# Retention attention inside a fused three-stage kernel: decay factors applied to the queries on GpSimd, outputs copied by ScalarE, the state recurrence as one scan, and one sequence of background weight pieces

## The chip, the cores and the metric

The kernel runs on one core of a Trainium2 chip. The metric is device time in microseconds (us) of one execution. TensorE multiplies matrices (PE in the profile, PEld for its weight loads), VectorE (DVE), ScalarE (ACT) and GpSimd (POOL) work elementwise, and SyncE (SP) issues most of the DMAs. Each engine takes its instructions in program order.

## The reference, cut to what matters

Three layers follow each other: attention with a decay, a gated layer (w_in, w_sg, w_out) and a two-matrix layer (w_ch1, w_ch2). B is 4, there are 8 heads, 576 positions, 64 features per head, 512 in all. The lines that the change touches:

```python
scores = scale * np.matmul(q, k.transpose(0, 1, 3, 2))
gamma = 1.0 - 2.0 ** (-5.0 - np.arange(H))
Dmat = np.where(rel >= 0, gamma[:, None, None] ** rel[None, :, :], 0.0)
attn = np.matmul(scores * Dmat, v)
h = gelu(x @ w_in);  u, v = halves of h;  v_n = layernorm(v) * g_ln
x = x + (u * (einsum(w_sg, v_n) + b_sg)) @ w_out
```

The decay is a power of gamma of the distance, so it splits into a factor of the query's position and one of the key's. The weights w_in, w_out and w_ch arrive as 64-bit floats and are turned into 32-bit ones on the chip.

## The kernel before, in words

**Attention.** A unit is one batch entry and one pair of heads: 16 units, `n` from 0 to 15. A unit's queries and keys (transposed), keys and values lie in one tile `ld` of 1120 KB with four buffers. Positions are cut into four chunks of 128 and a rest of 64. `prep_unit` scales the keys by their factors on ScalarE (L212). `scores` multiplies queries and keys on TensorE (L224, L236), and VectorE multiplies the scores by a mask with the keys' factors (L229, L237). `states` forms a key-value product for each chunk (L245) and the running state `y` over chunks: ScalarE copies the first (L251), three VectorE instructions, one behind the other, add the others (L253). `attend` adds both parts of the output on TensorE (L277, L284, L290), and VectorE multiplies it by the queries' factors `grow` on the way from PSUM to `xb` (L295, L300).

**Order.** The loop's iteration `n` issues the load of unit n+3, `prep_unit(n+2)`, `scores(n+1)`, `states(n+1)` and `attend(n)`. Between them stand `background` steps, three in an iteration from n = 2: `f64_pieces` loads 64-bit weights two pieces ahead (L134), converts a piece in four steps on VectorE (L142, L146, L149, L151) with a square on ScalarE (L148), and then splits it into a high and a low part (L310 on ScalarE, L311 on GpSimd) or stores it. w_in, w_sg, w_out and w_ch follow each other; w_out's pieces and w_ch's are two such sequences, and the second issues its first loads when the first has ended. Later the numbers in `PACE` say how many background steps stand behind each tile.

**The gated layer.** For each batch entry `b`, `v_tile` forms the tiles of v and `u_chunk` those of u (L124 to L126), with a gelu on ScalarE (L529) that counts a `tick`; `after(n, fn)` puts work n ticks later. A tile of v is normed (L514, L499, L519 to L523, L526) and split (L554, L555) for `sg_chunk`, which multiplies by w_sg. Where b is even there is a fifth tile, with the rests of two entries: after its norm (L526), two DMAs copy its lower half to `v_rest` (L587), a third overwrites that half (L588), and three ticks later it is split. Before each `u_chunk`, `turn_x` transposes a piece of `xb` on VectorE (L669) and stores it with four DMAs (L676). The tiles of v, the transposed pieces and the rows read back share five buffers `t`, in rotation.

All of these DMAs are issued by SP.

Of the kernel before, what the change touches and what calls it, by code (L numbers as in the profile page):

```python
# [3 lines left out]

# [1 line left out]

# [5 lines left out]
F32 = mybir.dt.float32  # L12
# [3 lines left out]
ALU = mybir.AluOpType  # L16
# [3 lines left out]
B, H, S, D = 4, 8, 576, 64  # L20
E = H * D
NP = H // 2
F1 = 1024
F2 = 2048
C = 128
NC = S // C
# [20 lines left out]
LATE = 6  # L47
# [15 lines left out]
O_GROW = O_MASKR + R  # L63
O_GK = O_GROW + C
O_GC = O_GK + 2
TA = O_GC + 1


O_GLN = 0
# [5 lines left out]
def const_tables():  # L75
    g = np.array(GAMMA, np.float64)
    p = np.arange(128)
    tab = np.zeros((NP, 128, TA), np.float64)
    for hp in range(NP):
        for h in range(2):  # L80
            gh = g[2 * hp + h]
            tab[hp, :, O_MASK + h * C:O_MASK + (h + 1) * C] = (np.arange(C)[None, :] >= p[:, None]) * gh ** -p[:, None]
            tab[hp, :, O_GK + h] = gh ** (C - p)
        gp = g[2 * hp + p // D][:, None]
        tab[hp, :, O_MASKR:O_MASKR + R] = (np.arange(R)[None, :] >= (p % R)[:, None]) * gp ** -(p % R)[:, None]
        tab[hp, :, O_GROW:O_GROW + C] = gp ** np.arange(C)[None, :] / np.sqrt(D)
        tab[hp, :, O_GC] = gp[:, 0] ** C
    return tab.astype(np.float32)


# [1 line left out]
def kernel(  # L92
# [27 lines left out]
    def col(t, o, n=1):  # L120
        return t[:, o:o + n]
# [37 lines left out]
    def bank():  # L159

        return banks.popleft()
# [38 lines left out]
    def prep_unit(n):  # L200
        u = units[n]
        hp = n % NP
        t = u["ld"]
        u["qT"] = t[:, 0:S]
        u["kT"] = t[:, S:2 * S]
        u["k"] = t[:, 2 * S:2 * S + NC * C].rearrange("p (c e) -> p c e", c=NC)
        o = 2 * S + NC * C
        v = t[:, o:]
        u["v"] = v
        for h in range(2):  # L210
            k = u["k"][:, :, h * D:(h + 1) * D]
            act.activation(out=k, in_=k, func=ACTF.Copy, scale=col(tab[hp], O_GK + h))  # L212
# [26 lines left out]
    def states(n):  # L239
        u = units[n]  # L240
        us = bank()
        for c in range(NC):
            for h in range(2):
                r = slice(h * D, (h + 1) * D)
                pe.matmul(  # L245
                    us[r, c * D:(c + 1) * D], u["k"][:, c, r],
                    u["v"][:, c * C + h * D:c * C + (h + 1) * D], start=True, stop=True,
                )

        y = u["y"] = pa.tile([128, NC, D], F32, tag="y", name="y")  # L250
        act.copy(y[:, 0], us[:, 0:D])  # L251
        for c in range(1, NC):
            dve.scalar_tensor_tensor(  # L253
                out=y[:, c], in0=y[:, c - 1], scalar=col(tab[n % NP], O_GC), in1=us[:, c * D:(c + 1) * D],
                op0=ALU.mult, op1=ALU.add,
            )
        free(us)

    def attend_rest(n):
# [8 lines left out]
    def attend(n):  # L268
        u = units.pop(n)
        b, hp = divmod(n, NP)  # L270
        grow = col(tab[hp], O_GROW, C)
        o = bank()
        rest, p, v, qT, y = u["rest"], u["p"], u["v"], u["qT"], u["y"]
        for c in range(NC):
            for h in range(2):
                r = slice(h * D, (h + 1) * D)
                pe.matmul(  # L277
                    o[r, c * C:(c + 1) * C], v[:, c * C + h * D:c * C + (h + 1) * D], p[:, h, c],
                    start=(c == 0), stop=(c == NC - 1), skip_group_check=True,
                )  # L280
        for c in range(1, NC):
            for h in range(2):
                r = slice(h * D, (h + 1) * D)
                pe.matmul(  # L284
                    o[r, c * C:(c + 1) * C], y[r, c - 1], qT[r, c * C:(c + 1) * C], start=False, stop=(c == NC - 1),
                    skip_group_check=True,
                )
        for h in range(2):
            r = slice(h * D, (h + 1) * D)
            pe.matmul(  # L290
                rest[r, 64:64 + R], y[r, NC - 1], qT[r, NC * C:], start=False, stop=True, skip_group_check=True
            )
        if hp == 0:
            xb[b] = xbp.tile([128, KE, S], F32, tag="xb", bufs=4, name="xb")
        dve.tensor_tensor(  # L295
            out=xb[b][:, hp, 0:NC * C].rearrange("p (c i) -> p c i", c=NC),
            in0=o.rearrange("p (c i) -> p c i", c=NC),
            in1=grow.unsqueeze(1).to_broadcast([128, NC, C]), op=ALU.mult,
        )
        dve.tensor_tensor(  # L300
            out=xb[b][:, hp, NC * C:], in0=rest[:, 64:64 + R], in1=grow[:, 0:R], op=ALU.mult
        )
        free(o)
        free(rest)

# [15 lines left out]
    def load_w_out():  # L321
        for k in range(KE):
            if k % 2 == 0:
                s = slot("w_out").rearrange("p (k a n) -> p k a n", k=2, a=2)
            t = s[:, k % 2]
            wo.append(t)
            yield (w_out[k], t[:, 0], t[:, 1])
# [21 lines left out]
    def f64_pieces(pieces, lead=2):  # L349

        pieces = iter(pieces)
        ahead = deque()

        def load():
            todo = next(pieces, None)
            if todo is not None:
                ahead.append((todo, f64_words(todo[0], 512)))

        for _ in range(lead):
            load()  # L360
        yield
        before = None
        while ahead:
            load()
            todo, raw = ahead.popleft()
            steps = f64_to_f32(raw, 512)
            next(steps)
            yield
            if before is not None:
                split(*before)  # L370
                before = None
            c = yield from steps
            if len(todo) == 3:
                before = (todo[1], todo[2], c)
            else:
                nc.sync.dma_start(out=todo[1], in_=c)
            yield
        if before is not None:
            split(*before)
# [37 lines left out]
    def background_steps():  # L417
        yield from f64_pieces(load_w_in(), 1)
        yield from load_w_sg()
        yield from f64_pieces(load_w_out())  # L420
        yield from f64_pieces(islice(w_ch_pieces, 2 * NF - LATE))

    bg = background_steps()

# [114 lines left out]
    def after(n, fn):  # L539
        late.append((step[0] + n, fn))  # L540
# [16 lines left out]
    def v_tile(b, i, ps=None):  # L557

        if ps is None:
            ps = v_products(b, i)  # L560
        if i == 0:
            vn[b] = tuple(big.tile([128, NC + 1, 512], F32R, tag=f"vn{a}", name=f"vn{a}") for a in "hl")
            if b % 2:
                after(1, lambda: iter([split_v(b, NC, v_rest[b])]))
        t = t1.tile([128, 512], F32, tag="t", bufs=NBT, name="t")

        st = numbers(t1)

        def norm_t():
            yield from squares(st, t, vn[b][0][:, i])  # L570

            def numbers_t():
                root(st, st[:, 1:2], 1.0 / 512, 1e-6)
                yield

            after(1, numbers_t)
            after(2, lambda: newton(st))

            def rest():
                normed(t, st)  # L580
                if i < NC:
                    split_v(b, i, t)
                else:

                    r = v_rest[b + 1] = t1.tile([128, 512], F32, tag="rest", bufs=1, name="v_rest")
                    for h in range(2):
                        nc.sync.dma_start(out=r[h * R:(h + 1) * R], in_=t[R:])  # L587
                    nc.sync.dma_start(out=t[R:], in_=t[0:R])  # L588
                    after(3, lambda: iter([split_v(b, i, t)]))
                yield  # L590

            after(3, rest)

        gelu(t, ps, ps, norm_t, st[:, 0:1])
        background(int(PACE[b][0][i]))
# [69 lines left out]
    def turn_x(b, i):  # L665

        n = 128 if i < NC else R
        t = t1.tile([128, 512], F32, tag="t", bufs=NBT, name="x_t")[:, 0:4 * n]
        dve.transpose(  # L669
            out=t.rearrange("p (q k c) -> p k q c", k=KE, c=32),  # L670
            in_=xb[b][:, :, i * 128:i * 128 + n].rearrange("p k (q c) -> p k q c", c=32),
        )
        at = 0 if i < NC else b % 2 * R
        to = x_dram[y_rows.index((b if i < NC else b | 1, i)), at:at + n]
        for q in range(4):
            nc.sync.dma_start(  # L676
                out=to[:, q * 128:(q + 1) * 128].rearrange("(a j) c -> j a c", j=32),
                in_=t[q * 32:(q + 1) * 32].rearrange("j (a c) -> j a c", c=128),
            )

    def load_x(b, i):
        x_rows[b, i] = t1.tile([128, E], F32, tag="t", bufs=NBT, name="x_r")
# [479 lines left out]
```

## Time and profile before

| | |
|---|---|
| time before, median of 3 runs | 700.74 us (699.19 to 702.92) |
| the profiled execution's own time | 702.03 us |
| its span in the profile | 700.2 us |
| TensorE busy | 668.7 us, 96% of the span |
| VectorE, ScalarE, GpSimd busy | 482.9, 303.2, 341.7 us |

Times in the profile count from the span's start; 1.83 us of the execution's own time lie outside the span. A row's "idle before" is time in which the engine had nothing running, with the work that ended most of it. A busy TensorE is not TensorE at its peak, since its matmuls overlap.

### The profile page before, as it was taken

Reading aid. Unit: us, or ns where it says so; the run is one execution under the profiler, and the core shown is the slowest. Engines: PE = TensorE matmul, PEld = TensorE weight load, DVE = VectorE, ACT = ScalarE, POOL = GpSimd, SP = SyncE. Lnnn points to the kernel's source line nnn. Section 1 sums busy time; section 2 is a strip of 40 time slices with the busy share of each in tenths; the row PEclk is TensorE's granted clock in tenths of the full one; section 3 lists DMA queues with packets and bytes.
Section 4 is the critical chain, followed back from the end, with each engine's and each line's share of the span. In section 5 each row is a group of like instructions: output and inputs, shape, how many; then the busy total and the mean of one; then the engine's idle time right before and its main releaser. Section 6 shows DMA issues by size and latency. Waiting matters only on the chain.

```text
span 700.2 us, 11668 instructions
## 1 busy us (share of the span) xinstructions
PE 668.7 (96%) x4294; PEld 594.4 (85%) x4294; DVE 482.9 (69%) x925; ACT 303.2 (43%) x584; POOL 341.7 (49%) x302
## 2 busy tenths in 40 slices
PE   6977997999999899999999999999999999999997
PEld 4866787989889789989888888888988888898985
DVE  2899775987997987686888676677656654433333
ACT  2344475345446436543444544343535433232221
POOL 0222445633622642993555498445448854445411
PEclk8999998999999999999999999999999999999999
DMA  8898635586596749535465523552641153121132
GB/s 323 288 353 301 201 108 161 155 277 198 167 306 206 226 153 259 161 129 208 166 181 169 147 76 106 186 164 93 190 122 61 64 189 124 61 97 69 30 121 90
DMA packets 61960, 116.96 MB, mean 167 GB/s; under 512 B 6480, under 2 KB 25936, under 8 KB 59984
## 3 DMA queue, kind: packets, MB, share of 16 engines
q1 hardware_dynamic: 61904, 116.23, 51.5%
q8 instruction: 33, 0.54, 0.3%
q14 instruction: 23, 0.19, 0.1%
HBM read 88.16 MB, written 27.26 MB: 165 GB/s over the span
## 4 chain that ended last, share of the span: by engine, by line
PE 55%; DVE 22%; DMA 7%; ACT 7%; issue 5%; POOL 3%; SPq 1%; DVEq 0%; ACTq 0%; POOLq 0%
PE b L124 16%; PE b L126 16%; PE b L125 16%; PE b L698 4%; DVE c L151 2%; DVE c L142 2%; DVE c L149 2%; DVE c L146 2%; DVE p L229 2%; DMA w_dram<-c 1%; DMA ld<-in_attn_dram 1%; DVE y L253 1%; DMA rows<-y_dram 1%; DVE xb L295 1%; DVE x_t L669 1%
## 5 line engine op out<-in xcount | busy, mean ns | idle before, releaser
L124 PE MATMUL b<-fe,w 128*128 128x384 f32 x336 | 114.6, 341 | 1.9 <-DVE h L967 1.1
L766 POOL TENSOR_TENSOR w<-raw_w,w 128x512 fp32r<-128x512 f32 x46 | 62.4, 1356 | 107.3 <-ACT w L765 104.3
L126 PE MATMUL b<-w,h 128*128 128x512 f32 x288 | 114.2, 396 | 0.0
L124 PE MATMUL b<-w,h 128*128 128x512 f32 x288 | 113.7, 395 | 0.0
L125 PE MATMUL b<-w,h 128*128 128x512 f32 x288 | 113.5, 394 | 0.0
L125 PE MATMUL b<-fe,w 128*128 128x384 f32 x336 | 113.3, 337 | 0.0
L126 PE MATMUL b<-fe,w 128*128 128x384 f32 x336 | 113.1, 337 | 0.0
L966 ACT ACTIVATE h<-b 128x384 fp32r<-128x384 f32 x72 | 35.3, 490 | 160.4 <-DVE b L994 122.2
L967 DVE SCALAR_TENSOR_TENSOR h<-b,h 128x384 fp32r<-128x384 f32 x72 | 40.0, 556 | 45.6 <-ACT h L966 45.6
L124 PEld LDWEIGHTS b<-fe,w 128*128 128x128 f32 x336 | 63.0, 188 | 9.5 <-DVE t L989 2.7
L752 POOL TENSOR_TENSOR w<-raw_w,w 128x768 fp32r<-128x768 f32 x23 | 45.8, 1993 | 48.3 <-ACT w L751 44.5
L125 PEld LDWEIGHTS b<-fe,w 128*128 128x128 f32 x336 | 63.1, 188 | 3.6
L126 PEld LDWEIGHTS b<-w,h 128*128 128x128 f32 x288 | 54.1, 188 | 13.1
L126 PEld LDWEIGHTS b<-fe,w 128*128 128x128 f32 x336 | 63.1, 188 | 0.0
L125 PEld LDWEIGHTS b<-w,h 128*128 128x128 f32 x288 | 54.1, 188 | 9.4
L124 PEld LDWEIGHTS b<-w,h 128*128 128x128 f32 x288 | 54.0, 188 | 8.7
L148 ACT ACTIVATE raw<-raw 128x512 f32<-128x512 f32 x44 | 29.9, 680 | 64.1 <-DVE c L146 58.9
L994 DVE TENSOR_TENSOR b<-b,u 128x384 f32<-128x384 f32 x48 | 26.9, 561 | 39.7 <-PE b L126 39.6
L751 ACT CAST w<-raw_w 128x1024 fp32r<-128x1024 f32 (+1 forms) x47 | 44.2, 943 | 12.7 <-POOL raw_w L742 8.0
L499 POOL TENSOR_TENSOR st<-st,par 128x1 f32<-128x1 f32 x36 | 23.0, 640 | 52.4 <-DVE st L498 52.1
L389 POOL TENSOR_TENSOR xt_lo<-xb,xt_hi 128x576 fp32r<-128x576 f32 x16 | 25.0, 1575 | 45.6 <-ACT xt_hi L388 41.4
L752 DVE TENSOR_TENSOR w<-raw_w,w 128x1024 fp32r<-128x1024 f32 x24 | 35.4, 1477 | 13.8 <-ACT w L751 13.8
(140 smaller groups left out, 1619.3 us busy)
## 6 DMA issues: line engine op xcount, KB each, us to landing
ld<-in_attn_dram SPq DMA_DIRECT2D x15, 1120.0 KB, 7.1
raw<-in_w_ch_dram SPq DMA_DIRECT2D x32, 512.0 KB, 4.9
raw_w<-w_dram SPq DMA_DIRECT2D x24, 512.0 KB, 3.8
raw_w<-w_dram SPq DMA_DIRECT2D x46, 256.0 KB, 2.6
w_dram<-c SPq DMA_DIRECT2D x32, 256.0 KB, 2.5
row<-y_dram SPq DMA_DIRECT2D x30, 256.0 KB, 4.4
x_r<-x_dram SPq DMA_DIRECT2D x18, 256.0 KB, 4.4
y_dram<-x_r SPq DMA_DIRECT2D x18, 256.0 KB, 3.0
```

Of the source, the lines that this page charges most:

```text
L124: pe.matmul(ps, lh, rh, start=first, stop=False, skip_group_check=True)
L125: pe.matmul(ps, lh, rl, start=False, stop=False, skip_group_check=True)
L126: pe.matmul(ps, ll, rh, start=False, stop=last, skip_group_check=True)
L148: act.activation(out=f(w1), in_=f(w1), func=ACTF.Square)
L389: pool.tensor_tensor(out=lo[:, k, 0:S], in0=xb[b][:, k], in1=f(hi[:, k, 0:S]), op=ALU.subtract)
L698: pe.matmul(ps, g, wo[k][:, w], start=done[0] == 1, stop=done[0] == 3 * KE, skip_group_check=True)
L751: act.copy(hi, r)
L752: (pool if s and part else dve).tensor_tensor(out=lo, in0=r, in1=f(hi), op=ALU.subtract)
L766: pool.tensor_tensor(out=t[:, 1], in0=raw, in1=f(t[:, 0]), op=ALU.subtract)
L966: act.activation(out=t[:, 0], in_=v, func=ACTF.Relu)
L967: dve.scalar_tensor_tensor(out=t[:, 1], in0=v, scalar=0.0, in1=f(t[:, 0]), op0=ALU.max, op1=ALU.subtract)
L994: dve.tensor_tensor(out=v, in0=v, in1=u, op=ALU.add)
```

## The change

- `prep_unit` multiplies the queries by `grow` in place, on GpSimd (on VectorE for unit 0, in two pieces), in one instruction over 512 columns and one over 64. `attend` then only copies its outputs, on ScalarE.
- `states` writes the products with the chunk as the innermost index, so that a feature's four chunks lie side by side in PSUM, and one `tensor_tensor_scan` of 256 elements forms all states. The factor of each step comes from the table, which grows from 451 to 706 columns per partition; `y` is read with a step of four elements by the matmuls of L284 and L290.
- w_out's pieces and w_ch's form one sequence.
- The three DMAs around `v_rest` are issued by ScalarE.
- The stores of `turn_x` are issued two ticks later.

```diff
-TA = O_GC + 1
+TA = O_GC + NC * D
...
-        tab[hp, :, O_GC] = gp[:, 0] ** C
+        tab[hp, :, O_GC:] = gp ** C * (np.arange(NC * D)[None, :] % NC > 0)
...
+        q, grow = u["qT"], col(tab[hp], O_GROW, C)
+        for x, y in ((0, 2), (2, NC)) if n == 0 else ((0, NC),):
+            part = q[:, x * C:y * C].rearrange("p (c i) -> p c i", i=C)
+            (pool if n else dve).tensor_tensor(
+                out=part, in0=part, in1=grow.unsqueeze(1).to_broadcast([128, y - x, C]), op=ALU.mult
+            )
+        (pool if n else dve).tensor_tensor(out=q[:, NC * C:], in0=q[:, NC * C:], in1=grow[:, 0:R], op=ALU.mult)
...
+        us_c = us[:, 0:NC * D].rearrange("p (e c) -> p c e", c=NC)
...
-                    us[r, c * D:(c + 1) * D], u["k"][:, c, r],
+                    us_c[r, c], u["k"][:, c, r],
...
-        y = u["y"] = pa.tile([128, NC, D], F32, tag="y", name="y")
-        act.copy(y[:, 0], us[:, 0:D])
-        for c in range(1, NC):
-            dve.scalar_tensor_tensor(
-                out=y[:, c], in0=y[:, c - 1], scalar=col(tab[n % NP], O_GC), in1=us[:, c * D:(c + 1) * D],
-                op0=ALU.mult, op1=ALU.add,
-            )
+        y = pa.tile([128, D * NC], F32, tag="y", name="y")
+        u["y"] = y.rearrange("p (e c) -> p c e", c=NC)
+        dve.tensor_tensor_scan(
+            out=y, data0=col(tab[n % NP], O_GC, NC * D), data1=us[:, 0:NC * D], initial=0.0, op0=ALU.mult, op1=ALU.add
+        )
...
-        dve.tensor_tensor(
-            out=xb[b][:, hp, 0:NC * C].rearrange("p (c i) -> p c i", c=NC),
-            in0=o.rearrange("p (c i) -> p c i", c=NC),
-            in1=grow.unsqueeze(1).to_broadcast([128, NC, C]), op=ALU.mult,
-        )
-        dve.tensor_tensor(
-            out=xb[b][:, hp, NC * C:], in0=rest[:, 64:64 + R], in1=grow[:, 0:R], op=ALU.mult
-        )
+        act.copy(xb[b][:, hp, 0:NC * C], o)
+        act.copy(xb[b][:, hp, NC * C:], rest[:, 64:64 + R])
...
-        yield from f64_pieces(load_w_out())
-        yield from f64_pieces(islice(w_ch_pieces, 2 * NF - LATE))
+        yield from f64_pieces(chain(load_w_out(), islice(w_ch_pieces, 2 * NF - LATE)))
...
-                        nc.sync.dma_start(out=r[h * R:(h + 1) * R], in_=t[R:])
-                    nc.sync.dma_start(out=t[R:], in_=t[0:R])
+                        act.dma_start(out=r[h * R:(h + 1) * R], in_=t[R:])
+                    act.dma_start(out=t[R:], in_=t[0:R])
...
-        for q in range(4):
-            nc.sync.dma_start(
...
+        def store():
+            for q in range(4):
+                nc.sync.dma_start(
...
+            yield
+
+
+        after(2, store)
```

## Rows read from the trace of the kernel before

**Rows 1.** The page's busy time (share of the span) by engine.

```profile
PE 668.7 (96%) x4294; PEld 594.4 (85%) x4294; DVE 482.9 (69%) x925; ACT 303.2 (43%) x584; POOL 341.7 (49%) x302
```

**Rows 2.** Windows of attention: length, busy time by engine, granted clock, DMA share, GB/s.

```profile
6.50:19.20 12.70, 9.47 (x109) 8.05 (x108) 4.53 (x12) 3.02 (x9) 0.00 (x0) 0.73 0.96 389
23.12:80.89 57.77, 48.82 (x870) 42.59 (x866) 55.84 (x126) 25.12 (x59) 17.50 (x14) 1.00 0.83 303
```

**Rows 3.** Timeline of TensorE: start, length, first matmuls of scores(1), (3), (4), (15).

```profile
12.43 2.08 PE L224 MATMUL b<-ld 64*128 64x128 f32 x16 [1.65 <-DMA ld<-in_attn_dram]
...
23.13 1.16 PE L224 MATMUL b<-ld 64*128 64x128 f32 x16
27.00 1.16 PE L224 MATMUL b<-ld 64*128 64x128 f32 x16
...
80.82 1.16 PE L224 MATMUL b<-ld 64*128 64x128 f32 x16
```

**Rows 4.** Chain of waits in one iteration: start, length of TensorE's pieces.

```profile
20.79 0.62 PE b L245 x16
...
22.28 0.80 PE b L284 x12
```

**Rows 5.** VectorE's groups of instructions from 23.12 to 80.89 us.

```profile
L253 DVE SCALAR_TENSOR_TENSOR y<-y,tab,b 128x64 f32<-128x64 f32 x34 | 9.5, 278 | 1.1
L295 DVE TENSOR_TENSOR xb<-b,tab 128x512 f32<-128x512 f32 x12 | 8.2, 684 | 0.4 <-PE b L284 0.4
L149 DVE SCALAR_TENSOR_TENSOR c<-raw,c 128x512 uint32<-128x512 uint32 x8 | 7.1, 894 | 0.1
...
L300 DVE TENSOR_TENSOR xb<-b,tab 128x64 f32<-128x64 f32 x12 | 2.6, 214 | 0.0
```

**Rows 6.** Groups of instructions: GpSimd over the span, ScalarE up to 110 us.

```profile
L311 POOL TENSOR_TENSOR w_in<-c,w_in 128x512 fp32r<-128x512 f32 x8 | 10.2, 1273 | 33.2 <-ACT w_in L310 33.2
L652 POOL TENSOR_TENSOR grem<-u,grem 128x64 fp32r<-128x64 f32 x16 | 9.0, 567 | 5.0 <-ACT grem L646 5.0
L529 ACT ACTIVATE t<-b 128x512 f32<-128x512 f32 x5 | 3.0, 598 | 2.1 <-PE b L126 2.1
```

**Rows 7.** DMA issues, median us to landing: 24 to 34, then 45 to 56 us.

```profile
ld<-in_attn_dram SPq DMA_DIRECT2D x2, 1120.0 KB, 7.6
...
ld<-in_attn_dram SPq DMA_DIRECT2D x3, 1120.0 KB, 6.1
```

**Rows 8.** Windows around the two later gaps of TensorE.

```profile
114.00:119.00 5.00, 1.16 (x9) 0.93 (x8) 2.76 (x7) 1.77 (x4) 1.49 (x2) 0.89 0.81 295
119.00:124.50 5.50, 5.00 (x20) 4.65 (x21) 5.05 (x8) 2.73 (x7) 1.45 (x2) 0.50 0.53 149
229.50:233.50 4.00, 1.07 (x4) 0.62 (x5) 3.90 (x7) 3.06 (x6) 3.26 (x2) 1.00 0.99 303
```

**Rows 9.** Timeline of SP's queue around the first gap, then at the second.

```profile
107.86 1.46 SPq L587 DMA_DIRECT2D v_rest<-t  x2
111.22 0.46 SPq L588 DMA_DIRECT2D t<-t  x1
...
224.13 1.11 SPq L587 DMA_DIRECT2D v_rest<-t  x2
227.00 0.46 SPq L588 DMA_DIRECT2D t<-t  x1
```

**Rows 10.** Timelines of ScalarE, VectorE and TensorE at the first gap.

```profile
107.43 0.39 ACT L529 ACTIVATE u<-b 128x288 f32<-128x288 f32 x1
...
111.27 0.41 ACT L529 ACTIVATE u<-b 128x288 f32<-128x288 f32 x1
113.42 0.62 ACT L554 CAST vnh<-t 128x512 fp32r<-128x512 f32 x1 [1.75 <-DMA t<-t]
...
115.67 0.43 DVE L142 TENSOR_SCALAR c<-raw 128x512 uint32<-128x512 uint32 x1 [7.49 <-DMA raw<-in_w_ch_dram]
...
118.76 0.61 PE L124 MATMUL b<-w_sg,vnh 128*128 128x288 f32 x1 [3.84 <-ACT vnh L554]
```

More of the change, by code (lines that the diff above doesn't have):

```diff
@@ L2 @@
 from contextlib import ExitStack
-from itertools import islice
+from itertools import chain, islice
 import numpy as np
@@ L270, in attend @@
         b, hp = divmod(n, NP)
-        grow = col(tab[hp], O_GROW, C)
         o = bank()
@@ L674, in turn_x @@
         to = x_dram[y_rows.index((b if i < NC else b | 1, i)), at:at + n]
-        for q in range(4):
-            nc.sync.dma_start(
-                out=to[:, q * 128:(q + 1) * 128].rearrange("(a j) c -> j a c", j=32),
-                in_=t[q * 32:(q + 1) * 32].rearrange("j (a c) -> j a c", c=128),
-            )
+        def store():
+            for q in range(4):
+                nc.sync.dma_start(
+                    out=to[:, q * 128:(q + 1) * 128].rearrange("(a j) c -> j a c", j=32),
+                    in_=t[q * 32:(q + 1) * 32].rearrange("j (a c) -> j a c", c=128),
+                )
+            yield
+        after(2, store)
     def load_x(b, i):
```

## The prediction, made before the change was run

> **What bounds the kernel now.** I read the busy shares first [rows 1]: TensorE is busy for 96% of the span, so the change can gain only where TensorE is idle or at the lower clock, and it can lose wherever it makes TensorE wait. Next I cut attention into stretches [rows 2]. From 23.12 to 80.89 us VectorE is busy for 55.84 of 57.77 us and TensorE for 48.82: here VectorE sets the pace. TensorE's timeline shows what that costs [rows 3]. Between scores(3) and scores(4), while the first four loads are still ahead, an iteration takes 27.00 - 23.13 = 3.87 us, which is TensorE's own pace. From 23.13 to 80.82 twelve iterations take 57.69 us, 4.81 each. So (4.81 - 3.87) x 12 = 11.3 us at most can be had there. DMA is not far away: 57.77 us at 303 GB/s are 17.5 MB, 1.46 MB an iteration, and at the 389 GB/s of the first stretch that takes 3.75 us [rows 2].
>
> After attention TensorE has two gaps that the change touches, where the gated layer waits for the last split tile of v, at 115 and at 229.5 us [rows 8, 10]. At the first it waits 3.84 us, and afterwards its granted clock is 0.50 (1.2 of 2.4 GHz) from 119 to 124.5 us, which is worth about 5.5 x 0.5 = 2.75 us. At the second it is busy for 1.07 of 4.00 us.
>
> I sum against the profiled execution's 702.03 us, which lies 1.29 above the median of the runs, and take 1.29 off at the end. A difference of 0.5% (3.5 us) is about what a measurement of this kernel can tell from no change.
>
> **The start.** scores(1) begin at 12.43, when unit 1 has landed [rows 3]. Two tables are ahead of that load, each longer by 255 x 4 x 128 = 130,560 bytes: 0.67 us at 389 GB/s [rows 2]. Then GpSimd must scale the queries before TensorE starts: one instruction over 512 columns like L311, 1.27 us, and one over 64 like L652, 0.57 us [rows 6]. Together +2.5 us. Without the second (if it were free) it is +1.9. Unit 0's own scaling, on VectorE, is 0.68 + 0.21 like L295 and L300 [rows 5]; it lies in TensorE's wait for unit 1. The iterations that follow run at TensorE's pace, so the delay is carried on: **+2.5**.
>
> **The steady iterations.** VectorE loses L253 (9.5 us), L295 (8.2) and L300 (2.6), 20.3 of its 55.84 us [rows 2, 5]. It gains twelve scans. No row shows a scan. Below, it costs what 256 elements cost on the line from L300 to L295: (684 - 214) / 448 = 1.05 ns an element, 0.42 us. Above, each element takes two steps, as 512 elements do: 0.68 us. I take 0.68, since each result must come back as an input, which now takes three instructions of 278 ns. The Trainium skill ("DVE: opcode table, instruction layouts, handler registers and perf-mode slots", section on the datapath and triggers) says that the built-in scan runs at half throughput; by it the estimate is the same 0.68 us, and the lower end would be out. VectorE then has (55.84 - 20.3 + 8.2) / 12 = 3.64 us an iteration.
>
> GpSimd gets 12 x 1.84 = 22 us beside the 17.5 it has. While it works, VectorE's conversions are slower: L149 takes 894 ns where an instruction of the same width takes 684 [rows 5]. Put on all four steps of 8 pieces that is 0.21 x 32 = 6.7 us with 17.5 us of GpSimd; 22 more would add 8.4, or 0.70 an iteration: VectorE 4.34 us. Bounds: nothing, 3.64; twice that, 5.04.
>
> The loads have a loop of their own. Unit n+3 is asked for when attend(n-1) ends, and its scores come two iterations later. In between it must land, 6.1 to 7.6 us [rows 7], and be scaled by GpSimd, 1.84. So two iterations are at least 7.9 to 9.4 us, one 3.97 to 4.72. VectorE's 4.34 and the middle of this, 4.35, agree: I take 4.35 us, (4.81 - 4.35) x 12 = **-5.5**. The ends are 3.87 (-11.3) and 4.81 (nothing). ScalarE takes two copies of outputs, 0.60 us (as L529 from PSUM [rows 6]) and a short one like the L251 that it loses; it has 25.12 us of work in 57.77 [rows 2]. That costs nothing, because an output's bank is not asked for until the iteration after next. Without that cover it would be 0.6 an iteration, 7 us.
>
> **Steps of four elements.** L245 now writes, and L284 and L290 read their weights, with a step of four. No row shows either on TensorE. Below: nothing. Above: twice the time, 0.62 us more for L245 and, where 0.80 us of L284 are twice as long in the weights but these already run beside its matmuls, perhaps 0.46 [rows 4]. I take nothing, since the conversions, transposes and splits of this kernel give no row in which an engine is slower by its step alone; the upper end is a rival below.
>
> **The DMAs of v_rest, on ScalarE.** SP's queue shows what the sequence lasts: issue at 107.86, and the third DMA's issue, which waits for the first two to land, ends at 111.68; at the second gap 224.13 to 227.46 [rows 9]. On ScalarE this stands in front of its other work. From 107.43 to 111.68 ScalarE runs eight instructions, 4.25 us, beside those DMAs, and then waits 1.75 for the third to land before it splits the tile at 113.42 [rows 10]. In the new order: issue 107.6 to 111.3, then 4 us of work, split at 115.4, +2.0 us. What waits: GpSimd's low part of it; then the buffer `t`, which VectorE's next transpose takes; behind that transpose on VectorE the last steps of the last tile's norm; then ScalarE's split of that tile, and TensorE. In return VectorE no longer waits for the first piece of w_ch. It waited 7.49 us [rows 10], but its transpose could not have begun before GpSimd's low part was done, at 113.42 + 0.62 + 1.27 (as L311) = 115.3, and it did begin when L142 ended, at 115.67 + 0.43 = 116.1: -0.7 with the ends' overlap. First gap: **+1.3**. At the second the same sequence holds ScalarE for 3.3 us, of which a part is hidden under the third DMA's flight: I take **+2.0**. Ends for both together: 0 and 2 x 3.8 = 7.6.
>
> **The rest.** One sequence of pieces brings the conversions one step forward and its loads two pieces earlier; beyond the 0.7 above its cover is TensorE's own work, and without that it would be a part of a step, under 1 us. The stores two ticks later: rows are read back a whole w_sg stage later, and SP comes free sooner for loads that TensorE does not wait for. Zero; if a store held a buffer, one landing of about 3 us.
>
> **Sum.** 702.03 + 2.5 - 5.5 + 1.3 + 2.0 = 702.3; less 1.29: **701.0 us**.
>
> **The rivals.**
> - *Loads and GpSimd keep up* (0.13): iterations of 3.95 us, -4.8 more, **696.2**. For it: 3.87 has been run [rows 3]. Against: landing takes 6.1 us or more [rows 7].
> - *ScalarE's wait is hidden and the first gap closes* (0.15): the +3.3 falls away, and 3.84 + 2.75 us come back [rows 8, 10]: 701.0 - 9.9 = **691.1**. For it: ScalarE is busy for 1.77 of 5 us at the gap. Against: the work queued behind those DMAs is what TensorE waits for.
> - *VectorE or the loads keep the old pace* (0.14): 4.81 stays, from the point where contention doubles or landing passes 7.8 us: 701.0 + 5.5 = **706.5**, slower.
> - *The steps of four cost* (0.15): iterations of 3.87 + 0.62 + 0.46 = 4.95 us; (4.95 - 4.35) x 12 + 4 x 1.08 = 11.5: **712.5**; at half the price 4.41, 12 x 0.06 + 4 x 0.54 = 2.9, **703.9**. It decides from about 0.5 us an iteration, where TensorE's own 3.87 passes the 4.35. The Trainium skill says just this ("SBUF — State Buffer", the note on cachelines): accesses of PSUM that are not contiguous slow matmuls significantly. No row here shows it.
>
> **How the numbers follow.** My forecast has 0.43. Faster than 697.2: 0.28, from the first two. Slower than 704.2: 0.30, from the other two and the forecast's edge. Between: 0.42. The range leaves out the lower half of the second rival and the upper half of the last: 693 to 709. The forecast's own range, by the ends of its loop (4.2 to 4.5) and of ScalarE's wait, is 698 to 704.5.
>
> **What would show it.** Iterations of L224 some 4.35 us apart, scores(1) near 15 us, VectorE with slack, a scan of 0.68 us; L245's sixteen matmuls still in 0.62 us; at the v_rest DMAs a ScalarE queue that stands still for 3 to 4 us, and TensorE's gaps longer by 1.3 and 2. It is wrong if L245, L284 or L290 are slower, if TensorE waits for GpSimd's scaling, or if the gaps shrink.

## The result and the profile after

The kernel after takes 709.11 us (median of 4 runs, 708.42 to 710.68), the kernel before 699.97 us beside it: a ratio of 1.0125, 95% interval 1.0108 to 1.0142, so 1.25% slower. The range was 693 to 709, and the time lies at its upper end, 0.1 us past it; the forecast of 701.0 missed it by 8.1. The likeliest case, no measurable change, did not happen. The profiled execution took 708.96 us with a span of 707.2, which is 7.0 more than the span of before.

The page's busy times of the kernel after:

```profile
PE 674.6 (95%) x4294; PEld 596.7 (84%) x4294; DVE 476.5 (67%) x864; ACT 311.2 (44%) x600; POOL 371.7 (53%) x332
```

Against [rows 1] GpSimd has 30 us more and VectorE only 6.4 less. The windows (length, busy time by engine in the order of [rows 1], granted clock, DMA share, GB/s) of the kernel after: steady attention; from there to the first product with w_sg's last row for b = 0, and on to that for b = 2; the two later gaps:

```profile
23.81:80.12 56.31, 49.97 (x866) 43.86 (x864) 53.78 (x80) 32.19 (x73) 41.88 (x37) 1.00 0.85 310
...
80.12:122.00 41.88, 37.38 (x277) 32.25 (x277) 21.28 (x51) 25.17 (x56) 22.02 (x20) 0.94 0.44 132
122.00:239.89 117.89, 109.93 (x634) 98.71 (x634) 99.28 (x207) 55.85 (x119) 48.35 (x46) 0.95 0.66 211
...
113.50:121.00 7.50, 3.60 (x11) 1.86 (x9) 0.74 (x1) 7.19 (x14) 5.64 (x5) 0.72 0.08 17
121.00:126.50 5.50, 4.91 (x20) 4.91 (x21) 5.36 (x9) 1.28 (x3) 0.54 (x1) 0.50 0.61 176
231.00:239.00 8.00, 3.07 (x8) 1.82 (x8) 6.35 (x11) 6.04 (x12) 5.07 (x4) 0.62 0.41 132
```

The two stretches behind attention in the kernel before:

```profile
80.82:120.52 39.70, 35.36 (x280) 31.37 (x277) 23.78 (x62) 23.93 (x51) 21.11 (x19) 0.97 0.46 139
120.52:233.60 113.08, 107.91 (x634) 97.58 (x633) 99.60 (x208) 56.16 (x119) 48.03 (x46) 0.98 0.69 219
```

Against [rows 2], GpSimd is busy 41.88 us in attention where it was 17.50, yet VectorE, relieved of 20.3 us of work and given 8.1 us of scans, is still busy for 53.78 of 56.31. Against [rows 8], TensorE is idle for 3.90 us at the first gap (3.84 before) and for 4.93 at the second (2.93 before). After the first its granted clock is 0.50 (1.2 of 2.4 GHz) for 5.5 us, as before, but it is already 0.72 in the gap (0.89 before), and at the second gap it is 0.62 where it was 1.00. Over both stretches TensorE is idle for 2.95 us more than before, (4.50 + 7.96) - (4.34 + 5.17), and busy for 4.04 us more with the same products: more of the loss comes from matmuls at the lower clock than from the idle time itself.

TensorE's timeline in the kernel after, with the first matmuls of scores(1), (2), (3), (15), and of the first products with w_sg's last row for b = 0 and b = 2:

```profile
14.18 1.90 PE L232 MATMUL b<-ld 64*128 64x128 f32 x16 [3.38 <-POOL ld L214]
...
19.75 1.16 PE L232 MATMUL b<-ld 64*128 64x128 f32 x16
23.81 0.38 PE L232 MATMUL b<-ld 64*128 64x128 f32 x2
...
80.12 1.05 PE L232 MATMUL b<-ld 64*128 64x128 f32 x14 [0.45 <-POOL ld L214]
...
122.00 0.44 PE L631 MATMUL b<-w_sg,vnh 128*128 128x288 f32 x1
...
239.89 0.45 PE L631 MATMUL b<-w_sg,vnh 128*128 128x288 f32 x1
```

Attention ends 0.7 us earlier than in [rows 3]. The products at 122.00 stood at 120.52 before, and those at 239.89 at 233.60: the loss is made behind attention, where the gated layer waits for the last tile of v. ScalarE's timeline in the kernel after, at the first gap and at the second:

```profile
107.22 1.17 ACTq L587 DMA_DIRECT2D v_rest<-t  x2
113.00 0.47 ACTq L588 DMA_DIRECT2D t<-t  x1
113.52 0.41 ACT L529 ACTIVATE u<-b 128x288 f32<-128x288 f32 x1 [6.33 <-DMA x_dram<-x_t]
...
119.02 0.62 ACT L554 CAST vnh<-t 128x512 fp32r<-128x512 f32 x1
...
225.82 1.13 ACTq L587 DMA_DIRECT2D v_rest<-t  x2
229.29 0.47 ACTq L588 DMA_DIRECT2D t<-t  x1
229.80 0.41 ACT L529 ACTIVATE u<-b 128x288 f32<-128x288 f32 x1 [4.02 <-PE b L126]
...
237.46 0.62 ACT L554 CAST vnh<-t 128x512 fp32r<-128x512 f32 x1
```

From the first of the three DMAs to the end of the third ScalarE does nothing else: 6.3 us at the first gap and 3.9 at the second, on SP's queue 3.8 and 3.3 [rows 9]. The releasers that L529's two rows name are not the cause. The third DMA may be issued only when the first two have landed, and all of ScalarE's work stands behind it, up to the last tile's split at 119.02 and 237.46. At the first gap ScalarE has no further wait between 113.52 and that split: what stood in its queue is what the split waits for. VectorE's timeline in the kernel after shows who waits for ScalarE:

```profile
120.25 1.83 DVE L151 SCALAR_TENSOR_TENSOR c<-raw,c 128x512 f32<-128x512 f32 x1 [9.61 <-ACT raw L148]
...
230.95 0.71 DVE L795 STREAM_TRANSPOSE rows<-rows 128x512 f32<-128x512 f32 x1 [4.70 <-ACT rows L526]
...
234.15 1.20 DVE L521 SCALAR_TENSOR_TENSOR st<-st 128x1 f32<-128x1 f32 x1
235.39 1.19 DVE L523 TENSOR_TENSOR st<-st 128x1 f32<-128x1 f32 x1
```

At the first gap this wait is a consequence and not on TensorE's way: VectorE's part of the last tile's norm is done at 110.04. At the second gap the wait goes through three engines: ScalarE's norm of a row tile comes late, VectorE's transpose of it (L795) waits 4.70 us, and behind that stand the last steps of the last v tile's norm, which ScalarE needs before its split at 237.46.

### The profile page after: what moved, and what is told of

Same layout as the page of the kernel before. It is cut to its first block, busy times and chain, and to the rows that moved or that the text cites. A ratio compares the mean times of both kernels' runs of the same rounds, so it can differ in the third digit from the quotient of the medians.

```text
span 707.2 us, 11677 instructions
## 1 busy us (share of the span) xinstructions
PE 674.6 (95%) x4294; PEld 596.7 (84%) x4294; DVE 476.5 (67%) x864; ACT 311.2 (44%) x600; POOL 371.7 (53%) x332
## 2 busy tenths in 40 slices
DMA packets 61962, 117.50 MB, mean 166 GB/s; under 512 B 6480, under 2 KB 25424, under 8 KB 59984
## 4 chain that ended last, share of the span: by engine, by line
PE 50%; DVE 19%; DMA 10%; ACT 8%; POOL 6%; issue 4%; SPq 1%; ACTq 0%; DVEq 0%; POOLq 0%
PE b L124 15%; PE b L126 15%; PE b L125 15%; DVE c L146 3%; DMA ld<-in_attn_dram 3%; PE b L704 2%; DVE c L151 2%; DMA w_dram<-c 2%; DVE c L149 2%; DVE c L142 2%; POOL gll L648 1%; DMA raw<-in_w_in_dram 1%; DMA v_rest<-t 1%; ACT t L526 1%; DVE p L237 1%
## 5 line engine op out<-in xcount | busy, mean ns | idle before, releaser
L151 DVE SCALAR_TENSOR_TENSOR c<-raw,c 128x512 f32<-128x512 f32 x44 | 40.0, 908 | 13.8 <-ACT raw L148 11.4
L124 PE MATMUL b<-w_sg,vnh 128*128 128x288 f32 x128 | 40.5, 316 | 6.2 <-ACT vnh L554 6.2
```

Of the source, the lines that this page charges most:

```text
L124: pe.matmul(ps, lh, rh, start=first, stop=False, skip_group_check=True)
L151: dve.scalar_tensor_tensor(out=f(c), in0=f(w1), scalar=F64_LEAST ** 2, in1=f(c), op0=ALU.is_ge, op1=ALU.mult)
```

## The experiments

Each kernel ran beside the kernel before on the same chip, whose medians there were 699.8 to 700.9 us; a difference of two medians of this table can be off by that much, the ratios are not. The stretches come from the profiled executions: scores(3); the mean of the twelve iterations from scores(3) to scores(15); from there to b = 0's first product with w_sg's last row (the first gap lies in it); on to that of b = 2 (it holds the second); and on to the span's end.

| kernel | median us | ratio, 95% interval | scores(3) | iteration | to b = 0 | to b = 2 | to the end |
|---|---|---|---|---|---|---|---|
| before | 699.97 | 1 | 23.13 | 4.81 | 39.70 | 113.08 | 466.6 |
| after | 709.11 | 1.0108 to 1.0142 | 23.81 | 4.69 | 41.88 | 117.89 | 467.3 |
| 1 v_rest on SP | 699.56 | 0.9975 to 1.0000 | 23.09 | 4.63 | 36.25 | 114.18 | 468.8 |
| 2 stores at once | 708.82 | 1.0105 to 1.0135 | 24.17 | 4.72 | 41.67 | 117.75 | 467.4 |
| 3 attention of before | 708.78 | 1.0105 to 1.0135 | 21.35 | 4.83 | 41.46 | 119.16 | 467.2 |
| 4 attention alone | 701.89 | 1.0007 to 1.0031 | 22.73 | 4.60 | 40.27 | 112.38 | 467.6 |
| 5 v_rest on ACT alone | 707.43 | 1.0088 to 1.0137 | 19.20 | 5.00 | 41.52 | 117.50 | 466.7 |
| 6 one sequence alone | 696.62 | 0.9925 to 0.9961 | 20.74 | 4.77 | 36.13 | 113.11 | 467.0 |
| 7 no query factors | 691.17 | 0.9848 to 0.9898 | 21.64 | 4.23 | 36.18 | 113.49 | 467.6 |
| 8 no scan | 697.04 | 0.9936 to 0.9972 | 22.41 | 4.90 | 35.74 | 115.02 | 467.2 |
| 9 factors after scores | 696.96 | 0.9932 to 0.9967 | 20.54 | 4.57 | 36.09 | 112.39 | 467.4 |
| 10 the same, no scan | 695.05 | 0.9905 to 0.9944 | 20.76 | 4.65 | 36.35 | 112.40 | 467.2 |
| 11 third DMA on SP | 705.08 | 1.0037 to 1.0087 | 23.11 | 4.72 | 38.47 | 114.92 | 467.1 |
| 12 kernel 10, split so | 699.74 | 0.9978 to 1.0005 | 20.08 | 4.73 | 38.16 | 114.48 | 467.0 |

The medians decide; a profile is one execution, and those of 4, 9 and 11 lie at the low end of their runs (700.00, 693.09 and 702.03 us), that of 8 at the high end (700.85).

### 1. The v_rest DMAs back on SP's queue

```diff
-                        act.dma_start(out=r[h * R:(h + 1) * R], in_=t[R:])
-                    act.dma_start(out=t[R:], in_=t[0:R])
+                        nc.sync.dma_start(out=r[h * R:(h + 1) * R], in_=t[R:])
+                    nc.sync.dma_start(out=t[R:], in_=t[0:R])
```

> The kernel after with the three transfers of every last tile's v rows issued on SyncE's queue again, as in the kernel before; the deferred stores, the one sequence of pieces, the scan, GpSimd's query factors and ScalarE's copies stay. Theory (ScalarE's place behind these transfers is the loss): ScalarE's stops of 6.3 us at 113.9 and 4.0 us at 230.2 go. The second gap, which grew by 5.7 us, returns to its length of before or a little more (SyncE's stores stand later now), and the first gap, which grew by 2.2 us, falls under its length of before because VectorE's wait of 7.49 us on the raw w_ch tile is gone: 709.1 - 5.7 - 0.8 - 2.2 - (0 to 6) = 694 to 701 us. Rival (the deferred stores or the one sequence make the gaps, whichever queue issues the v rows): no more than 2 us come back, 707 to 709 us.

699.56 us: 9.5 us come back, within the theory's range; the rival falls. This kernel's windows of the two stretches behind attention:

```profile
78.66:114.91 36.25, 35.24 (x277) 31.38 (x278) 22.65 (x51) 27.09 (x58) 22.46 (x20) 1.00 0.49 146
114.91:229.09 114.18, 107.42 (x634) 95.43 (x633) 98.28 (x207) 55.71 (x119) 48.52 (x46) 1.00 0.69 217
```

The first gap is nearly gone: TensorE is idle for 1.01 of 36.25 us, and the clock stays at 1.00. Of the 9.3 us that the two stretches give back, 4.7 are idle time and 4.65 are busy time of the same 277 and 634 matmuls, which ran at a mean granted clock of 0.94 and 0.95 in the kernel after. By the table the stretch to b = 0 is 3.4 us shorter than even in the kernel before: the change holds a gain that its own DMAs hid.

### 2. The stores at once

```diff
-        def store():
-            for q in range(4):
...
-        after(2, store)
+        for q in range(4):
...
```

> The kernel after with the output stores of a tile issued at once, as in the kernel before, and no longer two steps later; the v rows stay on ScalarE's queue. Theory (ScalarE stands still until the v rows have landed, whatever stores are in flight): ScalarE's two stops keep at least 4 us and 3 us, 706 to 711 us. Rival (the v rows land late because the deferred stores' transfers are issued just ahead of them): the stops fall to about 2.5 us, the landing time that these transfers had in the kernel before, and 699 to 704 us result.

708.82 us: the deferral of the stores is worth nothing that can be measured in this setting, as predicted, and does not explain the stops.

### 3 and 4. The attention of before in the kernel after, and the new attention alone

The diff of kernel 3 is the attention part of the diff of the change, reversed: factors, scan, layout, table and copies. Kernel 4 is the kernel before with that part alone. The first expectation speaks of seven instructions for the recurrence; there are three on VectorE and a copy on ScalarE.

> The kernel after with the attention section of the kernel before: VectorE applies the decay factors to the outputs, the recurrence is seven instructions per unit, GpSimd touches no queries, ScalarE copies no outputs. The v rows on ScalarE's queue, the deferred stores and the one sequence stay. Theory (the loss sits in the transfers behind attention): attention ends where it did before (0.7 us later than in the kernel after) and the gaps stay long, 708 to 712 us. Rival (the new attention pushes its lateness into the gaps): the gaps return to their lengths of before, 698 to 703 us.

> The kernel before with the new attention section alone: GpSimd's query factors, ScalarE's output copies, the scan. The transfers, stores and pieces are those of the kernel before. Theory (attention is worth its 0.7 us earlier end and nothing else): 698 to 700 us. Rival (new attention is itself a part of the loss behind it): 703 to 706 us. A third way, that attention's gain was eaten by the heavier stream of pieces and is larger alone: 694 to 697 us.

708.78 us, as the theory of kernel 3 has it, and 701.89 us, between the ranges given for kernel 4. The attention makes 0.3 us in the one setting and 1.2 in the other, both on the slow side and within what counts here as no change. The loss of 9 us is not there, and neither is the gain of 3 us that the prediction's first two terms promised. Kernels 1 and 6 give a third setting: they differ by the new attention and the later stores, and kernel 1 is 699.56 - 696.62 = 2.9 us slower, its interval clear of the other's. Their profiles put 0.6 of it before scores(15), 78.66 us against 78.02; what makes the rest behind attention is not shown.

### 5. The v_rest DMAs on ScalarE's queue alone

The reverse of experiment 1's diff, made in the kernel before.

> The kernel before with one edit: the three transfers of every last tile's v rows are issued on ScalarE's queue. Theory (this edit alone makes the whole loss, because ScalarE stands still until the rows have landed): about +8 to +10 us, 707 to 711 us, and ScalarE idle for 4 us or more at each of the two gaps. Rival (it needs the change's other edits, heavier traffic or later stores, to hurt; alone ScalarE stands still for the 3.3 us that SyncE's queue showed, and half of it is hidden): +2 to +4 us, 702.5 to 704.5.

707.43 us, against 700.93 of the kernel before on that chip: this one edit costs 6.5 us, less than the theory's 8 though within its 707 to 711, and the rival's 2 to 4 fall. In its profile ScalarE does nothing but these DMAs from 105.94 to 112.16 us, and TensorE's gaps are as long as in the kernel after. It costs 9.5 us where the one sequence is in place (experiment 1), since it also hides that edit's gain: with the DMAs on ScalarE the stretch to b = 0 is 41.5 us without the one sequence and 41.9 with it, with them on SP 39.7 and 36.1.

### 6. One sequence of pieces alone

```diff
-        yield from f64_pieces(load_w_out())
-        yield from f64_pieces(islice(w_ch_pieces, 2 * NF - LATE))
+        yield from f64_pieces(chain(load_w_out(), islice(w_ch_pieces, 2 * NF - LATE)))
```

> The kernel before with one edit: w_out's and w_ch's pieces in one sequence. Theory (this is the hidden gain of the change: VectorE's wait of 7.49 us on the first raw w_ch tile goes, and the first gap closes): first gap shorter by 3 us or more, 695 to 698 us. Rival (the gap is set by GpSimd's low parts and the norm anyway, as the prediction had it): 699.5 to 701 us.

696.62 us, 4.3 less than the 700.93 beside it, and the stretch to b = 0 is 3.6 us shorter: the theory holds. VectorE's timeline of this kernel, where [rows 10] had the wait of 7.49 us:

```profile
107.83 0.71 DVE L668 STREAM_TRANSPOSE x_t<-xb 128x512 f32<-128x512 f32 x1 [1.35 <-POOL vnl L554]
...
110.35 0.16 DVE L522 TENSOR_TENSOR st<-st 128x1 f32<-128x1 f32 x1
```

The transpose stands at 107.83 us, not at 116.1. It does wait for a low part of GpSimd's, but that of an earlier tile, and the last norm's last step is done at 110.5, in the kernel before at 117.2.

### 7. The query factors left out

The diff takes the five lines with `(pool if n else dve).tensor_tensor` out of `prep_unit` in kernel 1.

> The kernel after with the v rows on SyncE's queue, and with the multiplication of the queries by the decay factors left out (neither GpSimd nor, for unit 0, VectorE does it; so the attention outputs are those of unscaled queries). Theory (GpSimd's 1.5 + 0.5 us per unit stand in the loop of the loads and slow VectorE's conversions beside them): iterations of attention go from 4.63 us to 4.1 to 4.3, VectorE's four conversion steps from about 1.0 us back to 0.75 or less, and the start comes 1.5 to 2 us earlier: attention ends 5 to 8 us earlier, total 692 to 695. Rival (steps of four elements, or the loads' own bandwidth, set the pace): iterations stay above 4.5 us, total 697 to 699.

691.17 us, a little under the theory. VectorE's groups over the twelve iterations (count, busy, mean ns, idle before): first the kernel after, then this one.

```profile
L237 DVE TENSOR_TENSOR p<-b,tab 128x512 f32<-128x512 f32 x24 | 15.3, 678 | 2.1 <-ACT xt_hi L389 2.1
L146 DVE SCALAR_TENSOR_TENSOR c<-raw,c 128x512 uint32<-128x512 uint32 x8 | 10.2, 1276 | 0.1
L149 DVE SCALAR_TENSOR_TENSOR c<-raw,c 128x512 uint32<-128x512 uint32 x8 | 8.6, 1070 | 0.1
L262 DVE TENSOR_TENSOR_SCAN y<-tab,b 128x256 f32<-128x256 f32 x12 | 8.1, 675 | 0.0
L151 DVE SCALAR_TENSOR_TENSOR c<-raw,c 128x512 f32<-128x512 f32 x8 | 7.3, 916 | 0.3
L142 DVE TENSOR_SCALAR c<-raw 128x512 uint32<-128x512 uint32 x8 | 6.4, 796 | 0.0
```

```profile
L231 DVE TENSOR_TENSOR p<-b,tab 128x512 f32<-128x512 f32 x24 | 15.3, 679 | 2.5 <-ACT xt_hi L383 2.1 <-ACT raw L148 0.4
...
L149 DVE SCALAR_TENSOR_TENSOR c<-raw,c 128x512 uint32<-128x512 uint32 x8 | 7.6, 946 | 0.1
L146 DVE SCALAR_TENSOR_TENSOR c<-raw,c 128x512 uint32<-128x512 uint32 x8 | 7.5, 933 | 0.1
L151 DVE SCALAR_TENSOR_TENSOR c<-raw,c 128x512 f32<-128x512 f32 x8 | 7.2, 902 | 0.8 <-ACT raw L148 0.5
L142 DVE TENSOR_SCALAR c<-raw 128x512 uint32<-128x512 uint32 x8 | 3.6, 455 | 0.4 <-DMA raw<-in_w_in_dram 0.4
```

The four conversion steps cost 32.5 us with GpSimd's factors (31.7 in kernel 1) and 25.9 without, and the iteration falls from 4.63 to 4.23 us. So GpSimd's factors cost 8.4 us in all (699.56 - 691.17), for the 10.8 us of VectorE's that they replace (L295 and L300, [rows 5]).

### 8. No scan

```diff
-                    us_c[r, c], u["k"][:, c, r],
+                    us[r, c * D:(c + 1) * D], u["k"][:, c, r],
...
-        dve.tensor_tensor_scan(
...
+        act.copy(y[:, 0], us[:, 0:D])
+        for c in range(1, NC):
+            dve.scalar_tensor_tensor(
...
```

> The kernel after with the v rows on SyncE's queue and with the recurrence of the kernel before: one ScalarE copy and three VectorE instructions per unit in place of the scan, states side by side in PSUM and in the tile, so that no product reads weights or writes PSUM in steps of four, and with the short tables. Theory (the steps of four cost TensorE 0.19 us an iteration as weights, and the scan saves VectorE no more than 0.16): TensorE's own iteration falls from 4.06 to 3.87 us, weight loads from 204 to 138 ns, and the total stays within 1.5 us of 699.6, if anything under it. Rival (the scan is what relieves VectorE): iterations grow by 0.2 us or more, 702 us or more.

697.04 us, 2.5 under kernel 1 and one more than the theory allowed: the scan with its layout and tables is a loss here, not a relief. Where the 2.5 us lie the profile does not show: it is of an execution 3.8 us above the median, and its iterations are longer (4.90 us against 4.63), as the rival had them. The weight loads of an iteration without waits, of the kernel after and of this one (count, busy, mean ns), and the matmuls of the kernel after that write PSUM in steps of four:

```profile
L291 PEld LDWEIGHTS b<-ld,y 64*64 64x64 f32 x12 | 0.8, 203 | 0.2 <-issue 0.2
```

```profile
L291 PEld LDWEIGHTS b<-ld,y 64*64 64x64 f32 x12 | 0.6, 132 | 0.2 <-issue 0.2
```

```profile
L254 PE MATMUL b<-ld 128*64 128x64 f32 x16 | 0.7, 228 | 0.0
```

A candidate is the weights: reading them in steps of four takes 203 ns where 132 are enough, and TensorE's own iteration is 23.81 - 19.75 = 4.06 us in the kernel after, 3.87 in [rows 3].

### 9 and 10. The factors applied after the scores, with and without the scan

```diff
-tab ... gh ** -p[:, None]
+tab ... gh ** (np.arange(C)[None, :] - p[:, None]) / np.sqrt(D)
...
             scores(n + 1)
+            scale_q(n + 1)
```

The scores take the raw queries and the masks hold the whole decay; `scale_q` is the same GpSimd work, needed only by L291 and L297 an iteration later.

> The kernel after with the v rows on SyncE's queue, and with GpSimd's multiplication of a unit's queries moved behind that unit's scores: the scores take the unscaled queries, their masks hold the factors as well, and only the products with the states and the last chunk's read the scaled queries. GpSimd's work is the same. Theory (of what the query factors cost, the part on the path is TensorE's wait for GpSimd ahead of the scores, 4.4 us in the steady part and 1.7 us at the start; the slower conversions of VectorE are hidden behind it or come next): the waits for GpSimd go, iterations fall from 4.63 to about 4.35 us, the start comes about 1.5 us earlier, total 694.5 to 697. Rival (VectorE, slowed beside GpSimd, sets the pace as soon as the wait is gone): iterations stay at 4.55 us or more and only the start is gained, 697.5 to 699.5.

> As the kernel with the factors applied after the scores, and with the recurrence of the kernel before (a ScalarE copy and three VectorE instructions per unit) in place of the scan, so that no weights are read in steps of four. Theory (with the wait for GpSimd gone, TensorE's own 3.87 against 4.06 us and VectorE's 0.16 us longer recurrence cancel, and only the shorter tables help the start): within 1.5 us of that kernel. Rival (VectorE sets the pace and the chain of four instructions is longer for it): 2 us slower than that kernel or more.

696.96 and 695.05 us. TensorE's groups over the twelve iterations, first kernel 1, then kernel 9 (the last figures are idle time and what ended it):

```profile
L232 PE MATMUL b<-ld 64*128 64x128 f32 x192 | 13.9, 285 | 4.4 <-POOL ld L214 4.4
L284 PE MATMUL b<-p,ld 128*64 128x128 f32 x192 | 12.7, 274 | 0.9 <-DVE y L262 0.9
```

```profile
L224 PE MATMUL b<-ld 64*128 64x128 f32 x193 | 14.3, 285 | 0.1
L282 PE MATMUL b<-p,ld 128*64 128x128 f32 x192 | 12.9, 276 | 4.4 <-DVE y L260 4.3
```

The wait for GpSimd goes as the theory said, but a wait for VectorE takes its place and the iteration is 4.57 us: there the rival was right, and what is gained is the start. The total lies at the upper end of the theory's range. This profile is the fastest of kernel 9's runs, 3.9 us under their median, so its stretches flatter it. Kernel 10 is 1.9 us under kernel 9, a little more than its theory's 1.5, with overlapping intervals; its rival falls. At 0.9924 of the kernel before (0.9905 to 0.9944) it is the fastest version that computes the whole, though its interval meets those of kernels 6, 8 and 9: one line of the change, alone, does as well within what these runs can tell.

### 11 and 12. The first two DMAs on ScalarE's queue, the third on SP's

```diff
                         act.dma_start(out=r[h * R:(h + 1) * R], in_=t[R:])
-                    act.dma_start(out=t[R:], in_=t[0:R])
+                    nc.sync.dma_start(out=t[R:], in_=t[0:R])
```

> The kernel after with one line changed: of the three transfers of the last tile's v rows only the third, which overwrites rows that the first two still read, is issued on SyncE's queue again; the first two stay on ScalarE's. Theory (it is the third transfer's wait for the first two to land that stops everything behind it on ScalarE; issuing as such costs ScalarE only the 1.17 us that the profile shows): ScalarE's stops of 6.3 and 4.0 us go, 698 to 702 us, as with all three on SyncE's queue. Rival (ScalarE's part is small, and what hurts is that the first two land late on that queue, beside SyncE's 512-KB loads): the landing stays at 4 to 5 us and the gaps stay long, 705 to 709 us.

> The kernel with the factors applied after the scores and no scan, the fastest so far at 695.05 us, with the first two transfers of the last tile's v rows on ScalarE's queue and the third on SyncE's. Theory (ScalarE pays 1.2 us of issuing and SyncE's queue is held as long as before): 694 to 697 us, no difference that can be measured. Rival (ScalarE's 1.2 us lie on the way to the last split at both gaps): 697 to 699 us.

705.08 and 699.74 us. Kernel 11 took 701.89 to 707.88 us; its median is past the theory's range and at the lower edge of the rival's, whose reason is not there, since the first two land in 2.3 us. Kernel 12 lies on the rival's side. So the wait of the third DMA is only a part, 709.11 - 705.08 = 4.0 us; issuing the first two from ScalarE makes the rest, 705.08 - 699.56 = 5.5, and 699.74 - 695.05 = 4.7 in the other pair. With kernel 11's runs 6 us apart, which part is the larger is open. VectorE's timelines, kernel 10 and then kernel 12, show how 1.2 us of issuing grow:

```profile
106.97 0.71 DVE L669 STREAM_TRANSPOSE x_t<-xb 128x512 f32<-128x512 f32 x1 [1.34 <-POOL vnl L555]
...
108.24 1.22 DVE L521 SCALAR_TENSOR_TENSOR st<-st 128x1 f32<-128x1 f32 x1
109.49 0.16 DVE L523 TENSOR_TENSOR st<-st 128x1 f32<-128x1 f32 x1
```

```profile
108.18 0.71 DVE L669 STREAM_TRANSPOSE x_t<-xb 128x512 f32<-128x512 f32 x1 [2.68 <-POOL vnl L555]
...
109.44 1.22 DVE L521 SCALAR_TENSOR_TENSOR st<-st 128x1 f32<-128x1 f32 x1
110.69 1.19 DVE L523 TENSOR_TENSOR st<-st 128x1 f32<-128x1 f32 x1
```

A split on ScalarE, GpSimd's low part, the buffer that VectorE's transpose needs, the norm behind it and ScalarE again: each is 1.2 us later, and one more step of the norm falls beside GpSimd's work and takes 1.19 us in place of 0.16. TensorE loses 1.8 us at the first gap and 2.1 in the stretch to b = 2. These two profiled executions differ by 4.0 us in all, the medians by 4.7. Kernel 11's profile, at the low end of its runs, shows less than its median does.

## Where the prediction was right and where it failed, step by step

- **The start, +2.5: right on average.** scores(1) began at 14.18, +1.75 in this pair. The profiled execution of before was itself late: over profiles, scores(3) stand at 22.7 to 24.2 us with the new attention (after, 1, 2, 4, 11) and at 19.2 to 23.1 with the old (before, 3, 5, 6), means 23.4 and 21.1, a difference of 2.3.
- **The steady iterations, -5.5: wrong in size.** They took 4.69 us, not 4.35, and gave 1.4. The scan was right (0.675 against 0.68), and so was the slowing of the conversions (32.5 - 24.3 = 8.2 us against 8.4). What failed is that VectorE's 4.34 us was taken for the iteration: VectorE was busy for 53.78 / 12 = 4.48 us of 4.69, about the same share as before, and the loop of loads was longer than its middle (landing 7.0 and 8.5 us at the two places of [rows 7], and 2.07 of GpSimd's scaling, 1.54 and 0.54). Over the same profiles as above the iterations have means of 4.67 and 4.85 us, 2.2 us in twelve, which the later start takes back: the attention as a whole gains nothing (experiments 3 and 4). Experiments 7 and 9 show both limits: take the wait for GpSimd away and VectorE's comes up at once; take GpSimd's work away and the iteration is 4.23.
- **Steps of four, taken as nothing: half right.** As PSUM outputs they are free: L254's matmuls take 228 ns, as those of L245 do in the kernel before; the Trainium skill ("SBUF — State Buffer", the note on cachelines), by which they should slow matmuls significantly, is not borne out by these rows. As weights they cost 71 ns a load, and TensorE's own iteration is 0.19 us longer. That did not decide the sign. The times without the scan are 2.5 and 1.9 us lower (experiments 8 and 10); that these weights and the longer tables are the reason is argued and not shown, for the iterations in those profiles are not shorter.
- **ScalarE's copies: not seen to cost.** They were not tried alone.
- **One sequence, -0.7: wrong.** It is worth 4.3 us alone. The step that failed is "its transpose could not have begun before GpSimd's low part was done": that transpose's buffer was free far earlier (experiment 6).
- **The DMAs of v_rest, +1.3 and +2.0: the step that decided.** The mechanism, a ScalarE queue that stands still and all that is behind it, was right. The size was not: the stand lasted 6.3 and 3.9 us, not 3.7 and 3.3 (at the first gap the second DMA landed after 5.1 us where 2.4 had been enough), and the prediction let part of it hide. Against the gap without it (36.25 and 114.18) the kernel after pays 5.6 and 3.7 us, 9.3 of the 9.5 that experiment 1 gives back. At the first gap the prediction looked for the delay in a chain through the buffer and VectorE's last norm; that chain is over at 110.04, and the last split waits for ScalarE's queue alone. At the second it missed that ScalarE's norm of a row tile stands in the same queue and holds VectorE, and with it the last norm. And it put no price on the clock for the longer gaps: half of the 9.3 us is TensorE's work at the lower clock (experiment 1).
- **The stores: right** (experiment 2).

Among the rivals "ScalarE's wait is hidden and the first gap closes" saw a gain that is there, 4.3 us in kernel 6 where it put 3.84 + 2.75 for the gap, under the wrong condition: the gap closes when ScalarE is left alone (kernels 1 and 6). Neither of the rivals on the slow side named what made the kernel slower. The upper part of the range stood on those two, so that the time came out at its edge is luck.

## What to carry to other kernels

A DMA that must wait for another should not stand in the queue of an engine that computes; and before an engine is given even the issuing, follow its queue through every engine that it feeds, since 1.2 us became 2 at each gap here. Count with a longer wait of TensorE the lower clock that followed it, half of the loss here. Where work is moved from VectorE to GpSimd, price what VectorE's other instructions lose beside it, and keep the moved work off the loop that sets the pace. A change of several edits should be taken apart: one of these is worth -0.6% alone and another +1.1%, and where both are in place the gain of the first is gone.

## What the runs showed of the hardware

With all three DMAs on ScalarE's queue the second of the two v_rest transfers landed later: the two took 2.3 and 5.1 us, in the kernel before 2.2 and 2.4. The DMA issues of the first gap (count, size, median us to landing), in the kernels before, after and 11:

```profile
v_rest<-t SPq DMA_DIRECT2D x2, 128.0 KB, 2.3
```

```profile
v_rest<-t ACTq DMA_DIRECT2D x2, 128.0 KB, 3.7
```

```profile
v_rest<-t ACTq DMA_DIRECT2D x2, 128.0 KB, 2.3
```

SP's timeline in the kernel after:

```profile
107.93 0.35 SPq L134 DMA_DIRECT2D raw<-in_w_ch_dram  x1
109.58 1.74 SPq L678 DMA_DIRECT2D x_dram<-x_t  x4
```

On SP's queue the third DMA had also kept SP's next load and stores back until the first two had landed; with all three on ScalarE's queue SP issues a 512-KB load at 107.93 and stores at 109.58 beside them. With the third on SP again, and the first two still on ScalarE's queue, they land in 2.3 us.

VectorE is slowed beside GpSimd only in some instructions. L146, L149 and L151, with two operands in SBUF, take 1276, 1070 and 916 ns in the kernel after (840, 894 and 684 before); L237 and the scan, with one operand in PSUM, take 678 and 675 whatever GpSimd does, and a step over a single column can take 1.19 us in place of 0.16. Such a step can last until the GpSimd instruction beside it ends: in the kernel after 8 of the 36 L519 start while GpSimd is inside an instruction, and each ends within 0.02 us of that instruction's end, 0.38 to 1.66 us long; the other 28 take 0.18 to 0.22. The Trainium skill ("GPSIMD Engine Reference", Specifications) names VectorE's instructions with two SBUF inputs, or in a 2-port performance mode, as those that contend with GpSimd; the trace agrees for L146, L149, L151 and L237. L142, with one input in SBUF, also went from 621 to 796 ns; whether it runs in such a mode no run here shows.
